# Key turns written in a row and read with a step by ScalarE, x of unit 1 copied by ScalarE, weight sums and one plain product moved, in a sparse attention and feed-forward kernel

## The chip, the cores and the metric

The kernel runs on one core of a Trainium2 chip. A core has five engines that run side by side: TensorE (PE in the profile; its weight loads are PEld) multiplies matrices into the accumulator memory PSUM, VectorE (DVE) and ScalarE (ACT) read PSUM and work element by element, GpSimd (POOL) works on the main on-chip memory, and SyncE (SP) issues transfers. Transfers (DMA) are issued from SyncE, ScalarE and GpSimd. The metric is the time of one execution on the device, in microseconds (us).

## What is computed

Attention over four batches of eight heads, 768 positions of 64 values. Each query sees the keys less than 16 positions away and, for each block of 32 positions, one summary key (the maximum over the block) that stands for 32. The result x feeds two layers with a sigmoid gate between them.

```python
k_sum = k.reshape(B, H, nb, block, D).max(axis=3)
v_sum = v.reshape(B, H, nb, block, D).mean(axis=3)
scores_l = scale * np.matmul(q, k.transpose(0, 1, 3, 2))
mask_l = np.abs(pos[:, None] - pos[None, :]) < window
scores_s = scale * np.einsum('bhsd,bhnd->bhsn', q, k_sum) + np.log(block)
...
x = attn_out.transpose(0, 2, 1, 3).reshape(B * S, H * D)      # 3072 x 512
h = x @ w_in                                                  # w_in 512 x 2048
out = (h * (1.0 / (1.0 + np.exp(-1.702 * h)))) @ w_out        # w_out 2048 x 512
```

## The kernel before

A **unit** is half a batch, 384 positions; there are eight, u = 0 to 7. The heads are taken as four **pairs** p, so that a pair fills 128 rows. Every engine keeps the order in which the program is written (the wrapper at line 28 sees to that, so nearly every row of the profile names line 28): what stands behind a waiting instruction on its engine waits too. The order is written out by hand.

**Start (lines 933 to 1028).** Twelve loads bring the keys of all four pairs (`kf`, half from SP and half from ACT) and the first half of their queries (`qf`). The build gives each load one of eight completion counters in turn, so the ninth and later loads are issued only when the load that last had their counter has landed. `exp_soon` makes ScalarE load its table for the exponential ahead of its first use. Then, for each pair, `cast_k` makes bf16 rows `kb`; `k_turn` transposes them with six matmuls of 128x128 against the identity `ident` into a bank pair `ps_k`; `k_own` copies that to the key array (`kx`), on ScalarE; `k_max` takes block maxima on VectorE. A load row holds three neighbouring positions (JH = 3), so the matmul of index r yields every third position, and `k_turn` writes its columns three words apart in PSUM, which puts positions in order. `q_turn` and `q_copy` do the same with queries (`ps_q`, `qT`): in the first half with the same stepped write, in the second half with a write in a row and a stepped write by VectorE's copy. `s_turn` makes scores in `ps_s`, `s_exp` their exponentials; `b_turn` and `b_exp` those of the block keys; `av_near`, `av_blocks` and `v_norm` the attention output, which `x_turn` transposes. `warmth` and `busy` are filler matmuls (`ps_w`). The fills of w_in, the second half of the queries and w_out are issued by GpSimd between its casts.

**A unit's feed-forward.** `ff_in` multiplies x transposed (`xT`, two halves of two pairs) with 16 column tiles of `w_in` (`ph`), and ScalarE puts the gate on each (`gT`). `ff_out` multiplies back with `w_out` (`po`): 12 calls of four matmuls, called slots 0 to 11. In unit 0 the slots run part by part of w_out (part 0 for three row tiles, then part 1, ...), so part 3 fills slots 9 to 11, and after each of these ScalarE copies the tile to `osb`. `beside(1, slot)` puts unit 1's attention between the slots, by the table `plan0`: q is a query turn, s scores of a pair, v the values of two pairs (with four norms on VectorE in all), x the transposes of two pairs by `tx` into `ps_x` with a copy to xT. `w_sums(c)` makes four sums of quarter-blocks of w_out on VectorE (`ta`, `tb`) for the fast matrix product (seven products instead of eight) used from unit 2 on. PSUM banks for `ph`, `po` and `ps_x` come from one ring of four (`mm`), so a new tile waits until the copy of the old one is done.

**The last units (`ff_in_pairs`, line 702).** Units 6 and 7 also do the first layer with seven products, M1 to M7, each two matmuls, for five pairs of column tiles, mixed with ten plain products of four matmuls into a bank L (`plain`). X, Y and V are banks; M5(i) adds to the bank X that VectorE reads for M6(i).

Of the kernel before, what the change touches and what calls it, by code (L numbers as in the profile page):

```python
# [35 lines left out]
def kernel(  # L36
# [16 lines left out]
    NP = H // 2  # L53
# [6 lines left out]
    HALF = S // 2  # L60
    TH = NQ // 2
    JH = NJ // 2

    pe = _Ordered(tc, nc.tensor)
    dve = _Ordered(tc, nc.vector)
    act = _Ordered(tc, nc.scalar)
# [207 lines left out]
    def copy(eng, out, in_):  # L274
        if eng is act:
            act.activation(out=out, in_=in_, func=ACT.Copy)
        elif eng == "dve_alone":

            dve.tensor_reduce(out=out, in_=in_.unsqueeze(len(in_.shape)), axis=AX.X, op=ALU.max)
        else:  # L280
            eng.tensor_copy(out=out, in_=in_)
# [94 lines left out]
    def at(ap, start, dims):  # L376
        a = ap[:, start:start + 1]
        return bass.AP(tensor=a.tensor, offset=a.offset, ap=[a.ap[0]] + dims)
# [24 lines left out]
    st = {}  # L403

    def k_turn(p):
        src = cast.pop(("k", p))
        big = st["K", p] = psb.tile([128, 1024], F32, name="ps_k", tag="big")
        for half in range(2):
            for r in range(JH):
                pe.matmul(out=at(big, half * 512 + r, [[JH, 128]]),  # L410
                          lhsT=src[:, half, r].rearrange("p h d -> p (h d)"),
                          rhs=ident, start=True, stop=True)

    def own_keys(p):
        return flat_kx(p, 1)[:, 0:S]

    def k_own(p, eng):

        copy(eng, own_keys(p).rearrange("p (e c) -> p e c", e=2),
             at(st["K", p], 0, [[512, 2], [1, HALF]]))  # L420

    def k_max(p):
        dve.tensor_reduce(out=ks0[p], in_=own_keys(p).rearrange("p (n c) -> p n c", c=block),
# [278 lines left out]
    def ff_in_pairs(u, early):  # L702

        (b11, b21), (b12, b22) = xTT
        xs = castp2.tile([128, 4, 2, HALF], F16, name="xsum", tag="kb")
        t = [xs[:, m] for m in range(4)]
        big = [psb.tile([128, 1024], F32, name="pw_in", tag="big") for _ in range(2)]
        mm = [pmm.tile([128, 512], F32, name="px_in", tag="mm") for _ in range(4)]
        X, V = ([m[:, 0:HALF] for m in mm[n:n + 2]] for n in (0, 2))
        Y = [big[0][:, n:n + HALF] for n in (0, 512)]  # L710
        L = big[1][:, 0:HALF]

        def gelu(w, f, src):
            act.activation(out=gT[w % 2][:, f, :], in_=src, func=ACT.Gelu_apprx_sigmoid)

        def one(w, f, ps):
            for ko in range(KO):
                pe.matmul(out=ps, lhsT=w_in_sb[:, ko, f * 128:(f + 1) * 128], rhs=xT[w % 2][ko],
                          start=(ko == 0), stop=(ko == KO - 1))
            gelu(w, f, ps)  # L720

        def prod(ps, a, b, i, first=False):
            for k in range(2):
                pe.matmul(out=ps, lhsT=a[:, k, i], rhs=b[:, k], start=(first and k == 0),
                          stop=(k == 1), skip_group_check=True)

        ws = [wt["s"][:, n] for n in range(4)]
        hold = {}

        def f0(i):  # L730
            return 2 * (NI - WI + i)

        def M1(i):
            x = X[i % 2]
            prod(x, wt[0, 0], b11, i, True)
            dve.tensor_copy(out=Y[i % 2], in_=x)

        def M7(i):
            v = V[i % 2]
            prod(v, ws[2], t[2], i, True)  # L740
            hold[i] = attp.tile([128, HALF], F32, name="m7", tag="x2")
            copy(act, hold[i], v)

        def M6(i):
            x = X[i % 2]
            prod(x, ws[1], t[1], i)
            dve.tensor_add(V[i % 2], x, hold[i])

        def M2(i):
            y = Y[i % 2]  # L750
            prod(y, wt[0, 1], b21, i)
            gelu(u, f0(i), y)

        def M5(i):
            x = X[i % 2]
            prod(x, ws[0], t[0], i)
            hold[i, 2] = attp.tile([128, HALF], F32, name="c22", tag="a_sb")
            dve.tensor_add(hold[i, 2], x, hold[i])

        def M4(i):  # L760
            v = V[i % 2]
            prod(v, wt[1, 1], t[3], i)
            gelu(u, f0(i) + 1, v)
            gelu(u + 1, f0(i) + 1, hold[i, 2])

        def M3(i):
            x = X[i % 2]
            prod(x, ws[3], b22, i)
            gelu(u + 1, f0(i), x)

        n, rest = 2 * (NI - WI), list(range(2 * (NI - WI)))

        def plain():
            one(u + 1, rest.pop(0), L)

        for f, ps in zip(range(n), (Y[0], X[1], V[1], L, Y[1], X[1])):
            if f == 2:
                M1(0)
            one(u, f, ps)
        dve.tensor_sub(t[2], b22, b12)  # L780
        dve.tensor_add(t[1], t[2], b11)
        dve.tensor_sub(t[0], b12, b11)
        dve.tensor_sub(t[3], b21, t[1])
        M2(0)
        M7(0)
        plain()
        M6(0)
        for i in range(1, WI):
            M1(i)
            for f in (M7, M5) if i == 1 else (M5, M7):  # L790
                f(i if f is M7 else i - 1)
            M4(i - 1)
            M6(i)
            M3(i - 1)
            M2(i)
            plain()
            if i == 2:
                early(0, NI - WI)
        i = WI - 1
        M5(i)  # L800
        M4(i)
        early(NI - WI, NI)
        plain()
        M3(i)
        assert not rest
# [123 lines left out]
    def exp_soon():  # L929
        act.activation(out=gate[:, 1:2], in_=gate[:, 0:1], func=ACT.Exp)  # L930


    dve.memset(gate, 0.0)
    for p in range(NP):
        load_k(p)
        load_q(p, 0)
    exp_soon()
    clear0(dve)
    dve.tensor_copy(out=identx, in_=ident)
    dve.memset(vs[:, :, D:VC], float(block))  # L940
# [102 lines left out]
    for p in range(NP):  # L1043
# [8 lines left out]
             6: ["v0", "s2", "s3"], 8: ["x0"], 9: ["v1", "S0", "S1"], 11: ["x1", "S2", "S3"]}  # L1052

    plan0 = {-1: ["q0", "q1"], 0: ["q2"], 1: ["q3"], 2: ["s0", "s1"], 4: ["s2", "s3"],
             7: ["v0", "v1"], 9: ["x0"], 11: ["x1"]}

    w51 = vw[1].rearrange("p (j e) h c -> p j e h c", e=2)

    def beside(u, slot):
        b, half = u // 2, u % 2  # L1060
        for what in (plan0 if u == 1 else plan1).get(slot, ()):
            i = int(what[1])
            if what[0] == "t":
                tq1(i, dve if i % 2 else act)
            elif what[0] == "q":
                q_turn(i, 1)
                q_copy(i, dve, 1)
            elif what[0] == "s":
                scores(b, half, i)
                if half and i == NP - 1:  # L1070
                    gelu_soon()
            elif what[0] == "S":
                scores(b, 1, i)
                if i == NP - 1:
                    gelu_soon()
            elif what[0] == "v":
                values(b, half, i, u == 1)
            else:
                tx(i, half)

    for u in range(2):
        todo = {}
        if u == 0:
            for p in range(NP):
                todo.setdefault(12 + p // 2, []).append(lambda p=p: cast_q(dve, p, 1))
        else:
            def value_rows():
                vsum(1, range(NJ))
                block_sums()
                halo_dmas(w51, 0)  # L1090
                sum_dmas(w51, 0)
                load_kc(2, range(6, H))
                load_vc(2)
                load_qc(2)

            todo = {0: [lambda: tk(0, 1)], 3: [lambda: tk(1, 1)], 5: [lambda: v_odd(1)],
                    9: [value_rows], 10: [lambda: tk(2, 1)], 13: [lambda: tk(3, 1)]}
            ff_in(u, range(3))
        for nt in range(0 if u else N0, NT):
            if u == 0 or nt > 2:  # L1100
                ff_in(u, (nt,))
            for f in todo.get(nt, ()):
                f()
        exp_soon()
        if u == 0:
            beside(1, -1)
            load_qc(1)
            load_kc(2, range(6))
        order = [(ms, part) for ms in range(JH) for part in range(4)]
        if u == 0:  # L1110

            order = [(ms, part) for part in range(4) for ms in range(JH)]
        for i, (ms, part) in enumerate(order):
            ff_out(u, ms, part)
            beside(u + 1, i)
            if u == 0 and i in (4, 7, 10):
                w_sums(i // 3 - 1)
            if u == 1 and i == 2:
                w_sums(3)
            if u == 1 and i == 3:  # L1120
                for g in range(2):
                    xk(g, 2)
# [22 lines left out]
    for b in range(1, B):  # L1145
# [3 lines left out]
        u = 2 * b  # L1149
# [95 lines left out]
```

The softmax here doesn't subtract the row's maximum and nothing guards it: scores larger than these inputs give would overflow.

## Time and profile before

| what | value |
|---|---|
| median of 6 runs | 208.75 us (208.21 to 209.3) |
| the profiled execution | 208.72 us |
| its span, first to last instruction | 207.0 us |
| TensorE matmuls | 199.8 us busy, 2212 |
| VectorE | 145.5 us busy |
| ScalarE | 123.7 us busy |
| GpSimd | 91.6 us busy |
| granted TensorE clock | 1.000 |
| HBM read, written | 27.26 MB, 6.29 MB |

The busy rows are times in which an engine has at least one instruction in work, as a share of the span. The difference of 1.7 us between the execution's time and the span lies around the span. In a row of the chain of waits stand the start, the length, the engine and the tile; the chain is followed back from the last instruction, at each step to what released it.

### The profile page before, as it was taken

How to read it: one execution, taken by the hardware profiler on the slowest of the kernel's cores; microseconds unless marked ns; L12 is line 12 of the kernel's file. 1: busy time of each engine (PE TensorE's matmuls, PEld its weight loads, DVE VectorE, ACT ScalarE, POOL GpSimd, SP SyncE). 2: the span in 40 equal slices, each digit the busy share in tenths (PEclk: the TensorE clock that was granted, in tenths of full speed). 3: DMA queues.
4: the chain of work that ended last, by engine and by line, in shares of the span. 5: the costliest groups of instructions: out<-in, count | busy, mean ns of one | idle time of the engine just before them, and what ended most of it. 6: DMA issues, size and time to landing. Idle time of an engine off the chain costs nothing.

```text
span 207.0 us, 5570 instructions
## 1 busy us (share of the span) xinstructions
PE 199.8 (97%) x2212; PEld 136.5 (66%) x2212; DVE 145.5 (70%) x421; ACT 123.7 (60%) x235; POOL 91.6 (44%) x162
## 2 busy tenths in 40 slices
PE   7899999998999999999999999999999999999992
PEld 3657555545665656566888865567887855668882
DVE  6687845696966679945757689579985956669431
ACT  0877676734685389677743657677626477881220
POOL 5995889399899943425999100402000000000000
PEclk9999999999999999999999999999999999999999
DMA  6999999999999999999999997993064260000323
GB/s 181 298 165 207 245 249 217 174 155 231 153 167 133 150 128 114 185 162 148 114 127 206 136 274 142 111 180 62 3 127 104 48 183 0 3 2 25 105 76 101
DMA packets 95009, 28.94 MB, mean 140 GB/s; under 512 B 82880, under 2 KB 92000, under 8 KB 94984
## 3 DMA queue, kind: packets, MB, share of 16 engines
q0 software_dynamic: 67920, 14.88, 81.7%
q1 hardware_dynamic: 25432, 12.53, 31.3%
q10 hardware_dynamic: 1632, 1.18, 1.9%
q8 instruction: 17, 0.28, 0.6%
q14 instruction: 8, 0.07, 0.1%
HBM read 27.26 MB, written 6.29 MB: 162 GB/s over the span
## 4 chain that ended last, share of the span: by engine, by line
PE 90%; DVE 6%; ACT 1%; issue 1%; DVEq 0%
PE ph L28 30%; PE px L28 15%; PE pw L28 8%; PE po L28 7%; PE px_in L28 6%; PE ps_av L28 4%; PE ps_s L28 4%; PE py L28 4%; PE pw_in L28 4%; PE ps_w L28 2%; PE ps_k L28 1%; PE ps_t L28 1%; DVE ta L28 1%; PE ps_x L28 1%; DVE x L28 1%; PE ps_q L28 1%
## 5 line engine op out<-in xcount | busy, mean ns | idle before, releaser
L28 PE MATMUL ph<-xT,w_in_sb 128*128 128x384 f16 x384 | 65.4, 326 | 1.2 <-DVE xT L28 1.2
L28 PEld LDWEIGHTS <-w_in_sb 128*128 128x128 f16 x462 | 44.3, 98 | 30.2 <-issue 1.5
L28 ACT ACTIVATE gT<-ph 128x384 f16<-128x384 f32 x96 | 45.7, 491 | 21.0 <-PE ph L28 20.8
L28 PEld LDWEIGHTS <-gT 128*128 128x128 f16 x384 | 36.1, 98 | 11.8
L28 ACT ACTIVATE a_sb<-ps_s 128x768 bf16<-128x768 f32 x28 | 21.1, 806 | 8.8 <-PE ps_s L28 8.7
L28 PE MATMUL po<-w_out_sb,gT 128*128 128x512 f16 x96 | 23.4, 380 | 0.0
L28 PEld LDWEIGHTS <-ss 128*128 128x128 f16 x216 | 20.7, 98 | 2.6
L28 ACT ACTIVATE t<-px 128x256 f32<-128x256 f32 x21 | 8.1, 384 | 21.9 <-PE px L28 21.9
L28 DVE TENSOR_TENSOR a_sb<-a_sb,mk 128x768 bf16<-128x768 bf16 x28 | 15.2, 555 | 7.5 <-ACT a_sb L28 6.4
L28 PE MATMUL pw<-tb,gT 128*128 128x256 f16 x144 | 18.7, 273 | 0.0
L28 PE MATMUL px<-ta,ss 128*128 128x256 f16 x144 | 18.7, 273 | 0.0
L28 ACT ACT_TABLE_LOAD x10 | 12.8, 1283 | 5.8 <-DMA kf<-in_k_dram 5.7
L28 DVE TENSOR_TENSOR x<-ps_av,rc 128x384 f16<-128x384 f32 x28 | 15.6, 557 | 1.0
L28 POOL DMA_DIRECT2D vw<-in_v_dram x18 | 15.9, 931 | 0.0
L28 POOL DMA_DIRECT2D vw<-vw x12 | 6.5, 563 | 20.5 <-DVE vw L28 18.1
L28 POOL DMA_DIRECT2D kb<-in_k_dram x16 | 13.2, 856 | 3.6 <-DMA w_out_sb<-in_moe_w_out_dram 3.2
L28 POOL DMA_DIRECT2D qb<-in_q_dram x16 | 13.3, 929 | 0.6 <-DMA vw<-in_v_dram 0.5
L28 DVE TENSOR_TENSOR osb<-pw,t 128x256 f32<-128x256 f32 x18 | 7.5, 421 | 8.6 <-PE pw L28 5.3
L28 DVE TENSOR_TENSOR ss<-gT 128x384 f16<-128x384 f16 (+4 forms) x18 | 7.5, 418 | 5.1 <-ACT gT L28 5.0
L28 PEld LDWEIGHTS <-kx 64*128 64x128 bf16 x400 | 7.2, 95 | 5.2 <-issue 4.0
L28 DVE TENSOR_REDUCE ks<-kx 128x24 bf16<-128x768 bf16 x8 | 7.6, 948 | 4.1 <-DMA kx<-kb 3.9
L28 PE MATMUL ps_s<-qT,kx 64*128 64x64 bf16 (+3 forms) x400 | 9.1, 190 | 0.3 <-DVE qT L28 0.2
(120 smaller groups left out, 312.7 us busy)
## 6 DMA issues: line engine op xcount, KB each, us to landing
out_dram<-osb SPq DMA_DIRECT2D x18, 256.0 KB, 4.3
vw<-in_v_dram POOLq DMA_DIRECT2D x18, 128.0 KB, 5.4
w_in_sb<-in_moe_w_in_dram POOLq DMA_DIRECT2D x4, 512.0 KB, 10.9
w_out_sb<-in_moe_w_out_dram POOLq DMA_DIRECT2D x4, 512.0 KB, 20.2
kb<-in_k_dram POOLq DMA_DIRECT2D x16, 96.0 KB, 5.1
qb<-in_q_dram POOLq DMA_DIRECT2D x16, 96.0 KB, 6.6
out_dram<-osb SPq DMA_DIRECT2D x12, 128.0 KB, 1.7
vw<-vs POOLq DMA_DIRECT2D x6, 148.5 KB, 3.9
```

Of the source, the lines that this page charges most:

```text
L28: r = f(*a, **kw)
```

## The change

Four edits. The key turns of the start write each matmul's 128 columns in a row, and ScalarE's copy reads them with a step of 128 words and puts positions in order. ScalarE's table load for the exponential is issued before its last two loads instead of after them. In unit 0's output layer, the copies of unit 1's x go to ScalarE, the second of them (x1) and the first weight sums move one slot forward. In the last units, one plain product moves from ahead of M6(0) to behind it.

```diff
     def k_turn(p):
...
-                pe.matmul(out=at(big, half * 512 + r, [[JH, 128]]),
+                pe.matmul(out=big[:, half * 512 + r * 128:half * 512 + (r + 1) * 128],
                           lhsT=src[:, half, r].rearrange("p h d -> p (h d)"),
                           rhs=ident, start=True, stop=True)
...
     def k_own(p, eng):
-        copy(eng, own_keys(p).rearrange("p (e c) -> p e c", e=2),
-             at(st["K", p], 0, [[512, 2], [1, HALF]]))
+        copy(eng, own_keys(p).rearrange("p (e c r) -> p e c r", e=2, r=JH),
+             at(st["K", p], 0, [[512, 2], [1, 128], [128, JH]]))
...
         M2(0)
         M7(0)
+        M6(0)
         plain()
-        M6(0)
...
-    for p in range(NP):
+    for p in range(NP - 1):
         load_k(p)
         load_q(p, 0)
     exp_soon()
+    load_k(NP - 1)
+    load_q(NP - 1, 0)
...
     plan0 = {-1: ["q0", "q1"], 0: ["q2"], 1: ["q3"], 2: ["s0", "s1"], 4: ["s2", "s3"],
-             7: ["v0", "v1"], 9: ["x0"], 11: ["x1"]}
+             7: ["v0", "v1"], 9: ["x0"], 10: ["x1"]}
...
-                tx(i, half)
+                tx(i, half, act if u == 1 else dve)
...
-            if u == 0 and i in (4, 7, 10):
+            if u == 0 and i in (3, 7, 10):
                 w_sums(i // 3 - 1)
```

## The prediction

> **What bounds the kernel now.** I read the page's busy shares first, then who TensorE waited for, then the chain of waits through each place that came up, then tiles and transfers at those places.
>
> ```profile
> PE 199.8 (97%) x2212; PEld 136.5 (66%) x2212; DVE 145.5 (70%) x421; ACT 123.7 (60%) x235; POOL 91.6 (44%) x162
> ```
>
> ```profile
> PE ph L28 <- DVE xT L28: 1.2, 2, 0.8
> PE ps_k L28 <- DVE kb L28: 0.4, 1, 0.4
> PE ps_s L28 <- DVE qT L28: 0.2, 1, 0.2
> ```
>
> A TensorE at 97% says little (matmuls overlap and their ends are modelled). The waits say more: in 207 us TensorE waits for another engine four times after its first instruction (behind the arrow: sum, count, longest), and the largest sum is for xT on VectorE. So most of the kernel is TensorE's own stream, and time is to be had only where that stream is stretched. The chain shows three such places.
>
> ```profile
> 4.86 1.28 PE ps_k L28 x6
> 6.14 0.32 PE ps_w L28 x3
> ...
> 12.59 0.66 PE ps_k L28 x6
> ...
> 32.01 0.34 PE ps_q L28 x6
> ...
> 45.71 0.47 DVE xT L28
> ...
> 47.64 0.48 DVE xT L28
> ...
> 48.16 1.14 PE ph L28 x6
> ```
>
> First place, the start: six key turns take 1.28 us (213 ns each), while three filler matmuls of the same 128x128 shape right behind take 0.32 (107). Later, when TensorE runs at about twice the pace (the granted clock shows 1.0 throughout), six key turns take 0.66 (110) and six query turns of the second half 0.34 (57). What sets the two apart is the write: the slow ones write every third PSUM word, the fast ones a row. The half-0 query turns also write every third word (0.65 for three at 6.46) and stay so. Second place: from 37.9 to 48.2 us the chain leaves TensorE and runs on VectorE: masks, three weight sums of 1.5 us each, four norms, two copies of x. Third place:
>
> ```profile
> 170.61 0.34 PE px_in L28 x2
> ...
> 171.04 0.58 DVE px_in L28
> 171.66 1.62 PE px_in L28 x8
> ```
>
> Here a product of the last unit waits until VectorE has read the bank that it adds to.
>
> **The change, part by part.**
>
> *The plain product behind M6(0).* Matmuls follow each other every 0.163 us here. Before, starts are 171.09, 171.26, then 171.66 instead of 171.42: M5(0) adds to the bank that VectorE reads for M6(0) until 171.61. With the plain product's four matmuls (0.65) between them, M6(0) starts 0.65 earlier, VectorE's addition waits for ScalarE's m (170.06 + 0.48) and ends near 171.1, before 171.42. M6(0)'s input sum is ready at 169.24, before its new start at 169.79. The plain product is covered by nothing and costs nothing: the same four matmuls stand elsewhere. Gain **0.24**; what is late next is M3(0) (0.16, there already).
>
> *x copies to ScalarE, x1 and the first weight sums a slot earlier.* TensorE ends its transposes at 45.67 (45.34 plus six of 0.055) and could go on; it starts the input products at 46.23, and their second half at 48.16, not 47.21. Lost: 0.55 + 0.95 = **1.50**. In the changed order ScalarE runs, from 43.48: osb 0.60, x0 0.805, osb 0.60, x1 0.805, osb 0.60, so x0 is there at 44.89 and x1 at 46.29 at the latest. TensorE now does the x1 transposes before the last four output matmuls and starts the input products at the same 45.67; it needs x0 at once, and x1 and its bank for the third tile at 45.67 + 4 x 0.163 = 46.33. Both fit, x1 by 0.04. In the built order the bank of the third output tile, which is copied last, is not waited for until the fourth tile. VectorE must have the last norm done before x1's transposes at 44.5: norms start when the values are there (41.1) and take 4 x 0.69, so 43.8. The first weight sums (1.56) now stand before the masks of s2 and s3: these end near 40.4 rather than 40.0; the values that need them start at 41.1. The chunks of w_out that the sums wait for are there. Gain 1.45 to 1.50; **1.49** taken. If ScalarE were 0.3 slower, 0.26 of it is lost.
>
> Here a rule stands against the change. The Trainium skill, "ScalarE: Activation LUTs", section Rules for kernel authors, gives plain arithmetic to VectorE, "not ScalarE". The rows agree on the price:
>
> ```profile
> L28 ACT ACTIVATE xT<-ps_x x5: 472/492/805, 20.2 to 82.2; 128x384 f16<-128x384 f16 x3, 128x768 f16<-128x768 f16 x2
> L28 DVE COPY xT<-ps_x x5: 357/552/558, 22.0 to 74.7; 128x768 f16<-128x768 f16 x4, 128x384 f16<-128x384 f16 x1
> ```
>
> By the rule alone the two copies lose 2 x 0.25 = 0.5 us. But ScalarE is idle 2.55 before its first osb and 2.5 after the last, and VectorE is the chain, so I go by the chain: +1.49, not -0.5.
>
> *Key turns in a row.* TensorE saves 6 x 0.106 = 0.64 on the first pair and 6 x 0.053 = 0.32 on each of three others. Not all of it lies on the path, as VectorE is busy without a break from 7.1 to 14.0. The first query copy on VectorE moves from 7.14 to 6.50; but the next cast needs a load issued at 1.84 that takes 5.3, so at 7.14, where it started at 7.61. The cast after it took 1.32 instead of 0.35, and ended at 9.20 just after GpSimd's issue of the v loads (to 9.01). If it is held to 9.2 again, VectorE gains nothing there, and what remains is TensorE's own: three turns of pair 2 (0.16), six of pair 3 (0.32), less small waits: 0.37 by 15.5 us. If it slips through, the stage is up to 1.4 shorter. Either way a ceiling waits:
>
> ```profile
> w_out_sb<-in_moe_w_out_dram POOLq DMA_DIRECT2D x1, 512.0 KB, 17.0
> ```
>
> Issued at 14.73, it lands at 31.73; the first output product starts at 32.18. That leaves 0.45. I take **0.40** for the start.
>
> *The strided read on ScalarE.* No row shows ScalarE reading PSUM with a step. Contiguous it takes 811 ns for 768. Bounds: no change (a gain has no reason), or twice, 1.6 us. The second is the rule of "PSUM — Partial Sum Buffer", Specifications, that lines have 8 bytes and broken patterns slow matmuls much, carried over to a reader; the trace shows it for TensorE's writes (107 to 213). But TensorE's strided writes reach a word per 0.86 ns (110 for 128), and ScalarE reads no faster when contiguous: its rows of 1024 and 768 elements, 1024 and 806 ns, differ by 0.85 ns an element. So I take no change. At 1.6, ScalarE's row of four copies and three exponentials becomes the path: the first stage then ends 0.2 later than before instead of 0.4 earlier.
>
> *The table load before the last two loads.* ScalarE's first key copy can start near 6.05 (its last issue) instead of 7.08; the scores behind it wait for the query copy too, so I count nothing. The price is order: the build lets a ninth load wait for an earlier one's landing, and which one changes. k of pair 3 now waits until 5.23 (was issued at 4.08), q of pair 3 until about 5.65 (5.27). Landing 5.7 and 5.9 later: 11.0 and 11.55. VectorE casts that k at 12.02: 1 us of cover. GpSimd casts that q at 11.20: 0.35 late, and its w_in, q and w_out issues after it. They then lie 10 to 21 us in a full queue, so I cost this at 0; without that cover the 0.45 above shrinks to 0.1.
>
> **Sum.** 0.40 + 1.49 + 0.24 = 2.13. The profiled execution took 208.72 (span 207.0 and 1.7 around it); the median of the runs is 208.75, so no correction: **206.6**. Later transfers allow it: the last v rows for the block sums land near 52.4 (needed 54.4 - 1.9), the sum rows at 65.0 (67.5 - 1.9), the transposed queries at 96.7 (100.0 - 1.9).
>
> **The rivals.** *Loads are the floor.* The page shows the DMA at 9 in nearly all slices to 135 us, and margins of 0.1 to 0.6 above are thin; against it, TensorE waits for no load now. The start's 0.4 is lost and 0.2 at 52: 207.2. *ScalarE at twice the price*: 1.73 - 0.2, so 207.2. *Slower*: ScalarE's strided read costs far more than twice. Its fourth key copy ends at about 8.1 + 4c for a cost c (6.05, a cast, two exponentials, four copies); the block scores of pairs 2 and 3 at 17.9 need it 0.94 earlier. The loss passes the 1.73 gained elsewhere from c = 2.65, over three times the row; at four times (3.2) it is 4.1 lost, 211.1. Nothing in the trace speaks for that much. *It doesn't do what it says*: the gap at 46 to 48 stays, because x1 on ScalarE comes behind the osb copies; then 208.1.
>
> **How the numbers follow.** Forecast 0.66 (206.2 to 207.0); loads 0.10; twice 0.10; gap stays 0.06; slower 0.05; and 0.03 for a tie between. A measurement of this kernel tells 0.2% (0.4 us) from no change. All but the last two cases are faster, 0.92; I move 0.02 of it to slower for what I don't see: faster 0.90, within 0.03, slower 0.07. Range 205.9 to 207.5: below, the start comes through whole if w_out lands earlier; above, both middle rivals.
>
> **What would show it.** Six key turns at 0.34 when fast; key copies on ScalarE at 0.81; no wait of ph for xT; starts 0.163 apart at M5(0); first po 0.4 earlier, and if it waits for w_out, the ceiling. Wrong if key copies exceed 1.6 us, or TensorE waits for loads between 50 and 100 us.

## The result, and the profile after

| | before | after |
|---|---|---|
| median of all runs | 208.7 us (208.13 to 209.51, 38 runs) | 207.41 us (206.39 to 210.38, 17 runs) |
| the profiled execution | 208.72 us | 207.41 us |
| its span | 207.0 us | 205.7 us |

The ratio is 0.9934, with a 95% interval of 0.9919 to 0.9948: 1.4 us gained (1.1 to 1.7), where the forecast said 2.1. The median, 207.41, lies inside the range of 205.9 to 207.5, but only 0.1 under its upper end. The ratios here and below leave out a few longer runs with a lower granted clock (0.984 to 0.992), and are not exactly those of the medians. The busy line of the changed kernel, and four lines of its list of what TensorE waited for:

```profile
PE 197.2 (96%) x2212; PEld 134.4 (65%) x2212; DVE 143.3 (70%) x419; ACT 124.9 (61%) x237; POOL 91.4 (44%) x162
```

```profile
PE ps_k L28 <- DVE kb L28: 1.0, 3, 0.4
PE ps_av L28 <- issue: 0.6, 1, 0.6
PE ps_q L28 <- POOL qb L28: 0.5, 1, 0.5
PE ps_av L28 <- DMA vw<-vs: 0.5, 2, 0.3
```

The wait of `ph` for `xT` (1.2 before) is gone. The waits of the key turns for `kb` grew from 0.4 to 1.0. Four entries are new. Two are at the start: for queries that GpSimd casts (`qb`), and for keys that ScalarE copies (`kx`, 0.4, not shown). `issue` is a stall that no other engine ends. The last is a wait of TensorE for a transfer, which the profile before does not have: the values of unit 1 (`ps_av`) wait for the rows of v's block sums (`vw<-vs`, called the sum rows from here on).

The places in order of time. First the start: the six key turns of pair 0 and of pair 3, from the timeline of TensorE of the changed kernel (start, length, operation).

```profile
4.40 0.63 PE L28 MATMUL ps_k<-ident,kb 128*128 128x128 bf16 x6
4.87 0.33 PE L28 MATMUL ps_w<-warm 128*128 128x128 bf16 x3
...
11.52 0.60 PE L28 MATMUL ps_k<-ident,kb 128*128 128x128 bf16 x6
```

Six turns now take 0.47 us from their first start to the next instruction's. Before it was 1.19 (4.66 to 5.85):

```profile
4.66 1.49 PE L28 MATMUL ps_k<-ident,kb 128*128 128x128 bf16 x6
5.85 0.61 PE L28 MATMUL ps_w<-warm 128*128 128x128 bf16 x3
```

Not all of this is the edit. In this execution TensorE's pace had already doubled: the three fillers behind the key turns last 0.33, before 0.61. In e1, the same kernel in another execution, the fillers still start 0.107 apart, and the six turns take 0.64 (4.66 to 5.30). At the same pace the write in a row thus saves 0.55. The last pair begins 0.86 earlier than before (11.52 and 12.38), and the last scores of the start (`s_turn(3)`) 1.03 earlier (14.49 and 15.52). Little of this arrives:

```profile
18.34 0.54 PE L28 MATMUL ps_av<-vb,a 128*128 128x65 bf16 x13 [0.62 <-issue]
...
31.35 0.50 PE L28 MATMUL ps_q<-ident,qb 128*128 128x128 bf16 x6
31.96 1.04 PE L28 MATMUL po<-w_out_sb,gT 128*128 128x512 f16 x4
```

After the stall (in brackets) the lead is 0.49: the query turns start at 31.35, before at 31.84. The first output product starts at 31.96 instead of 32.18, so 0.22 is left. It follows the query turns by 0.61 where it followed by 0.34 before: w_out's first quarter, issued at 14.53, landed 17.4 later, at 31.93.

At the gap everything came as forecast. The timeline of TensorE of the changed kernel:

```profile
44.25 0.50 PE L28 MATMUL ps_x<-identx,x 128*128 128x128 f16 x6
44.58 1.03 PE L28 MATMUL po<-w_out_sb,gT 128*128 128x512 f16 x4
45.44 2.11 PE L28 MATMUL ph<-xT,w_in_sb 128*128 128x384 f16 x12
47.39 0.50 PE L28 MATMUL ps_t<-ident,kb 128*128 128x128 bf16 x6
```

The transposes of x1 stand before the last output product, and twelve input products run in a row, with no bracket. The key transposes behind them start at 47.39; before, at 49.13:

```profile
49.13 0.50 PE L28 MATMUL ps_t<-ident,kb 128*128 128x128 bf16 x6
```

The lead grows from 0.22 to 1.74.

Then part of it is lost. The chain of waits of the changed kernel in the stretch from 54 to 68 us:

```profile
55.93 6.29 DMA kq<-in_k_dram
...
62.85 3.53 DMA vw<-vs
66.38 0.14 issue
66.52 0.54 PE ps_av L28 x22
67.06 0.46 PE ps_s L28 x24
```

Here the chain no longer runs on TensorE. GpSimd issues the second half of the sum rows at 62.85, after a wait of 1.65 for a key load of batch 2 that it issued at 55.93; before, it issued them at 61.64. They land at 66.38 (before 65.04), and the values need them 1.7 earlier than before. That wait is not the whole cause: the first half, issued at 60.53 as before (60.54), took 5.5 to land instead of 4.3, so at 66.0 it is late too. TensorE loses 0.71 here.

Last, the plain product behind M6(0), on TensorE:

```profile
168.44 0.81 PE L28 MATMUL px_in<-xsum,wsum 128*128 128x384 f16 x4
169.09 0.81 PE L28 MATMUL pw_in<-xT,w_in_sb 128*128 128x384 f16 x4
169.74 0.49 PE L28 MATMUL px_in<-xT,w_in_sb 128*128 128x384 f16 x2
170.06 0.81 PE L28 MATMUL px_in<-xsum,wsum 128*128 128x384 f16 x4
```

All starts are 0.16 apart per matmul; the gap at M5(0) is gone, and the lead grows by 0.30. The sum over the places is 0.22 + 1.52 + 0.30 - 0.71 = 1.33, which is the difference of the spans (207.0 - 205.7 = 1.3).

### The profile page after: what moved, and what is told of

The parts are those of the page before. It is cut to its first block, busy times and chain, and to the rows that moved or that the text cites. A ratio compares the mean times of both kernels' runs of the same rounds, so it can differ in the third digit from the quotient of the medians.

```text
span 205.7 us, 5570 instructions
## 1 busy us (share of the span) xinstructions
PE 197.2 (96%) x2212; PEld 134.4 (65%) x2212; DVE 143.3 (70%) x419; ACT 124.9 (61%) x237; POOL 91.4 (44%) x162
## 3 DMA queue, kind: packets, MB, share of 16 engines
HBM read 27.26 MB, written 6.29 MB: 163 GB/s over the span
## 4 chain that ended last, share of the span: by engine, by line
PE 66%; DMA 21%; POOL 9%; issue 1%; SPq 0%; DVE 0%; POOLq 0%
PE ph L28 20%; PE px L28 16%; DMA w_out_sb<-in_moe_w_out_dram 10%; PE pw L28 8%; PE px_in L28 6%; DMA w_in_sb<-in_moe_w_in_dram 4%; PE py L28 4%; PE pw_in L28 4%; POOL qb L28 3%; DMA kq<-in_k_dram 3%; PE ps_av L28 3%; POOL vw L28 3%; PE ps_s L28 2%; PE po L28 2%; DMA qf<-in_q_dram 2%; POOL vb L28 2%
## 5 line engine op out<-in xcount | busy, mean ns | idle before, releaser
L28 PE MATMUL pw<-tb,gT 128*128 128x256 f16 x144 | 18.7, 273 | 0.0
L28 PE MATMUL px<-ta,ss 128*128 128x256 f16 x144 | 18.7, 273 | 0.0
L28 POOL DMA_DIRECT2D vw<-vw x12 | 6.5, 561 | 19.0 <-DVE vw L28 15.2
L28 DVE RECIPROCAL rc<-ps_av 128x6 f32<-128x6 f32 x32 | 6.0, 188 | 5.7 <-PE ps_av L28 5.4
## 6 DMA issues: line engine op xcount, KB each, us to landing
vw<-vs POOLq DMA_DIRECT2D x6, 148.5 KB, 4.5
```

Of the source, the lines that this page charges most:

```text
L28: r = f(*a, **kw)
```

## The experiments

Theory from this reading: the three edits do on TensorE what was forecast, but **transfers** take back about 0.7 to 0.9 us, at w_out's first quarter (32 us) and at the sum rows (66 us). Rivals: the start's gain is lost to TensorE's own stall at 18.3 us; or the forecast gains were not there at all, and only one of the edits works. In the tables the ratio is to the runs of the kernel before on the same chip (medians 208.98 beside e1 to e4, 208.79 beside e5 to e8, 208.77 beside e9 to e12).

### The sum rows on another queue: e1 to e4

e1 is the changed kernel again; e2 and e3 issue the sum rows and their neighbours from SP, in the changed kernel and in the one before:

```diff
-                halo_dmas(w51, 0)
-                sum_dmas(w51, 0)
+                halo_odd(w51, 0, sp)
+                halo_even(w51, 0, sp)
+                sum_dmas(w51, 0, sp)
                 load_kc(2, range(6, H))
```

e4 is e2 with the load of the second half of the queries cut in two, w_out's first quarter issued between the halves, and the casts of pairs 2 and 3 moved behind the query copies:

```diff
-    for p in range(NP):
-        load_q(p, 1)
-    for c in range(4):
+    load_q(0, 1)
+    load_q(1, 1)
+    load_w_out(0)
+    load_q(2, 1)
+    load_q(3, 1)
+    for c in range(1, 4):
         load_w_out(c)
```

> The changed kernel unaltered, as the measure for the three kernels beside it. Theory (late rows): near 207.4, and its times scatter by 1 us and more, since TensorE waits near 66 us for rows of v that pass through a full transfer queue. Rival (plain noise): the same 207.4, but the scatter has no wait in the profile that goes with it.

> The changed kernel with the six transfers of the halo and sum rows of unit 2's v issued by SP instead of GpSimd, where they stood behind six key loads and waited for one of them to land. Late rows: the wait of 0.7 us at slot 6 of unit 1 goes, the time falls to about 206.7, and the scatter shrinks to that of the kernel before (about 1 us over all runs instead of 2). Rival (all transfers share the same engines and are the floor): the rows land as late as before or the key loads behind them do, and the time stays within 0.2 of the changed kernel.

> The kernel before with the same six transfers on SP. Late rows: TensorE did not wait there before (rows at 65.0, needed at 67.5), so nothing is gained: 208.7, within 0.2. Rival (SP is just the better queue for these rows, or GpSimd's queue relieved of them speeds the loads behind): 208.2 or less.

> As the one with rows on SP, and the load of the second half of the queries split in two, with the first quarter of w_out between the halves, and the casts of pairs 2 and 3 behind the first two query copies. Theory (w_out's first quarter is the ceiling of the start): it lands about 2 us before it is needed, the first output product starts at 31.7 instead of 31.96, and the time is 0.25 lower than with rows on SP alone. Rival (the start's gain is lost before, near 18 us, where TensorE stood 0.6 us for nothing that shows): no change, within 0.1. It is slower by up to 0.5 if the later casts of the queries hold up the third query turn.

| | median us (runs) | ratio, interval | TensorE's waits for transfers in the profile |
|---|---|---|---|
| e1 | 207.88 (10) | 0.9933, 0.9907 to 0.9959 | w_out 1.1 |
| e2 | 208.52 (22) | 0.9969, 0.9950 to 0.9988 | w_out 1.5 |
| e3 | 209.34 (14) | 1.0010, 0.9988 to 1.0032 | w_out 0.4, sum rows 0.2 |
| e4 | 208.22 (22) | 0.9965, 0.9945 to 0.9985 | sum rows 0.9 |

The repeat has the same ratio, but not the same profile: this execution did not wait for the sum rows, it waited at w_out.

The remedy missed its expectation: in e2 the wait for the sum rows is gone, and the time is not better than e1's, by its median worse. The wait at w_out in e2 lies over 20 us ahead of the moved rows, so the edit did not put it there; and with TensorE late by it (values at 67.12), this profile does not test whether the rows come earlier. e4 does. There the wait for w_out is gone and the first output product starts at 31.7, as expected, but the wait for the sum rows is back at 0.9, though they are issued from SP. From the chain of e4:

```profile
58.63 8.75 DMA vw<-vs
```

SP issued the second half 4 us earlier than GpSimd did in the changed kernel (62.85), and it landed 1.0 later, at 67.38: it was under way for 8.75 us instead of 3.53. In e3 it was 9.07. Why rows from SP take longer was not tried. A limit that all transfers share would fit, and is not shown by this.

Two more things follow. One profile is one sample: where loads land differs between executions of the same program. And e3 shows no gain from the rows on SP where TensorE is not ahead.

### One edit at a time: e5 to e9

e5 has the edits of the start alone, e6 those of x and the weight sums alone, e7 the plain product alone; e9 is e6 and e7 together. e8 is the changed kernel with the copies of unit 1's x back on VectorE:

```diff
-                tx(i, half, act if u == 1 else dve)
+                tx(i, half)
```

> The kernel before with the key turns in a row, the stepped read on ScalarE and the earlier table load, and nothing else. Ceiling theory: TensorE is about 1.0 us ahead at 14.5 us, but the first output product waits for w_out's first quarter, so 0.2 to 0.3 is left at 32 us and at the end: 208.45. Rival (the start comes through): 207.7.

> The kernel before with unit 1's x copied by ScalarE, x1 and the first weight sums a slot forward, and nothing else. Theory: the gap of 1.5 us at 46 to 48 closes, ScalarE's copies show 0.80, and since TensorE is 1.5 and not 1.74 ahead at slot 6 of unit 1, it waits there 0.3 to 0.5 for the sum rows: 207.4 to 207.6. Rival (the rows land on time when the start is not moved): 207.2.

> The kernel before with the one plain product moved behind M6(0). Theory: M5(0) no longer waits, 0.25 to 0.3 less, nothing behind it can eat it: 208.45. Rival (a wait takes its place at M3(0) or at the bank L): 208.7.

> The changed kernel with the two copies of x back on VectorE, x1 and the weight sums still a slot forward. If ScalarE's copies carry the gain: the gap comes back whole, 208.7 or so. If the order carries it: VectorE ends the norms at 43.8 and the second weight sums at 45.3, then copies x0 by 45.9 and x1 by 46.4, so TensorE waits 0.45 for x0 and not for x1: up to 0.45 over the changed kernel, less if the wait for the sum rows behind it takes part of it up (it would then be within 0.2).

> The kernel before with the edits of x, the weight sums and the plain product; the start (key turns, table load) is that of before. If the start brings nothing because loads and a stall take it up: 207.4, as the changed kernel, ratio to before 0.992 to 0.995. If the start brings the 0.40 that was forecast: 207.8, ratio 0.9955. Expected 207.45.

| | edits | median us (runs) | ratio, interval |
|---|---|---|---|
| e5 | start | 208.87 (14) | 0.9995, 0.9973 to 1.0017 |
| e6 | x and weight sums | 207.76 (22) | 0.9951, 0.9931 to 0.9971 |
| e7 | plain product | 208.62 (14) | 0.9995, 0.9975 to 1.0014 |
| e8 | all, x copied by VectorE | 207.50 (15) | 0.9935, 0.9915 to 0.9954 |
| e9 | all but the start | 207.58 (22) | 0.9941, 0.9921 to 0.9961 |

The start alone brings nothing that can be measured; nor does its absence cost anything that can: e9 is at 0.9941 where the whole change is at 0.9934. The intervals, about half a microsecond either way, do not exclude the 0.40 that was forecast. The edit of x carries the gain, 1.0 us of the 1.4. The plain product alone (0.1 us by its ratio) is below what its interval can tell.

e8 says which half of that edit it is. With the copies on VectorE and only the order changed, two lines of its list of waits are

```profile
PE ps_av L28 <- DMA vw<-vs: 0.3, 1, 0.3
PE ph L28 <- DVE xT L28: 0.3, 1, 0.3
```

Of the 1.2 for `xT`, 0.3 is left. The time is the changed kernel's. So the **order** (x1 ahead of the last output product, the weight sums ahead of the masks) makes the gain; its two moves were not tried apart. The move to ScalarE is worth at most the remaining 0.3 on TensorE, and nothing of it shows in the times.

The start, seen over all these profiles. w_out's first quarter is issued at the same place in the program in all of them (in e4 it is not, and it is left out); issue and landing are from the list of that tile's instructions. The first three columns of times follow TensorE: the last scores of the start, the matmul at which it goes on after the stall near 18 us, and the query turns ahead of the first output product.

| start of | profile | last scores | goes on | query turns | w_out issued | lands | first output product |
|---|---|---|---|---|---|---|---|
| before | before | 15.52 | 18.83 | 31.84 | 14.7 | 31.7 | 32.18 |
| | e6 | 15.23 | 18.59 | 31.61 | 14.7 | 31.5 | 31.94 |
| | e3 | 15.05 | 18.61 | 31.62 | 15.3 | 32.4 | 32.50, waited 0.4 |
| | e7 | 15.25 | 18.59 | 31.61 | 15.5 | 32.8 | 32.81, waited 0.7 |
| | e9 | 15.18 | 18.32 | 31.42 | 15.5 | 32.9 | 32.90, waited 1.0 |
| after | after | 14.49 | 18.34 | 31.35 | 14.5 | 31.9 | 31.96 |
| | e5 | 14.90 | 18.32 | 31.33 | 14.9 | 31.3 | 31.67 |
| | e8 | 14.45 | 18.34 | 31.35 | 15.2 | 31.6 | 31.69 |
| | e1 | 14.30 | 18.09 | 31.10 | 15.0 | 32.6 | 32.69, waited 1.1 |
| | e2 | 14.57 | 18.34 | 31.34 | 15.4 | 33.2 | 33.30, waited 1.5 |

By the medians of the five profiles each, the new start leads by 0.74 at the last scores (14.49 and 15.23), by 0.25 behind the stall (18.34 and 18.59), and by 0.27 at the query turns (31.34 and 31.61). So most of its gain is lost at the stall, before any wait for a transfer. What is left meets a landing that goes from 31.3 to 33.2, whichever start the kernel has, and cannot be seen through that.

The stall is at the same matmul in all 14 profiles, those of before and of e10 to e12 included: behind the third of a block of values, where starts otherwise lie 0.03 apart, 0.10 to 0.85 us pass. In each of them a 16 KB packet of the kind `instruction` (the first on queue q8) has landed 1.2 to 1.5 us before TensorE goes on. It landed between 16.7 and 18.7, and TensorE went on between 18.1 and 20.1, later where the packet was later. In five profiles with the new start (after, e2, e4, e5, e8) it went on at 18.32 to 18.34, whether it had started the third matmul at 17.49 or at 17.94: coming earlier gained nothing. A wait for instructions to be loaded would fit. The profile does not say whose instructions the packet holds, and no run moved it, so the cause is not shown.

### Fewer bytes, and another order of loads: e10 to e12

If transfers take the gain back, it must come out where there are fewer of them. e10 and e11 leave out one load, 768 KB, ahead of w_out in the queue, in the kernel before and in the changed one:

```diff
-            if half:
-                pool.dma_start(out=early[1].rearrange("p i h r d -> p (i h) (r d)"),
-                               in_=q[0, :, HALF:S].rearrange("h (p r) d -> p h (r d)", r=JH))
...
-             raw["q", p, half])
+             raw["q", p, 0])
```

e12 computes everything, and moves the first six key loads of batch 2 behind the sum rows:

```diff
             load_qc(1)
-            load_kc(2, range(6))
...
                 sum_dmas(w51, 0)
-                load_kc(2, range(6, H))
+                load_kc(2)
```

> The kernel before without the load of the second half of batch 0's queries (768 KB); the casts for that half read the first half's queries, so that half of the output is another. At the mean 195 GB/s these bytes take 4 us, so what is queued behind them (w_out, the rows of unit 1) should land some 4 us earlier until the queue has caught up. In the profile of before TensorE waits for no load, so both theories expect no change here: 208.7, at most 0.4 less.

> The changed kernel with the same load left out. Theory that loads are the floor: TensorE no longer waits for the sum rows at 66 (0.7) nor stands near w_out at 32 (0.2 and more), and the whole forecast appears: 206.5, 2.1 under e10. Rival, that the start's gain is lost to TensorE's own stall at 18.3 and the rest is not due to loads: 207.2 to 207.5, 1.3 under e10.

> The changed kernel with six heads' key loads of batch 2 (384 KB as bf16, 768 KB read) issued behind the sum rows of unit 1 and no longer ahead of them. Theory that the sum rows waited for these loads: GpSimd issues the rows at about 61.2 without a wait, they land near 65, the wait at 66 (0.7) is gone and w_out's landing at 32 is not touched, since these loads are issued behind it: 206.8, ratio 0.990. Rival, that the wait only moves, to the key or query rows of batch 2 at 80 to 100 us: 207.4 as the changed kernel.

| | median us (runs) | ratio, interval |
|---|---|---|
| e10 | 208.72 (14) | 1.0000, 0.9975 to 1.0026 |
| e11 | 206.74 (6) | 0.9899, 0.9870 to 0.9928 |
| e12 | 206.97 (7) | 0.9921, 0.9889 to 0.9953 |

The kernel before doesn't notice the missing load, within half a microsecond. The changed one gains by it: e11 is 1.98 us under e10, close to the 2.13 of the forecast's sum. (The one profile of e10 is its slowest execution, 210.15 us; no time is read from it but those of the stall.) The list of waits of e11:

```profile
PE ps_k L28 <- DVE kb L28: 0.8, 2, 0.6
PE ps_av L28 <- issue: 0.5, 1, 0.5
PE ps_q L28 <- POOL qb L28: 0.5, 1, 0.5
PE ps_s L28 <- DVE qT L28: 0.4, 1, 0.4
PE ps_s L28 <- ACT kx L28: 0.4, 1, 0.4
```

No transfer stands in it, and the stall at 18 us does, at 0.51. The timeline of TensorE in e11 at the three places:

```profile
31.43 1.03 PE L28 MATMUL po<-w_out_sb,gT 128*128 128x512 f16 x4
...
43.73 0.50 PE L28 MATMUL ps_x<-identx,x 128*128 128x128 f16 x6
...
65.26 0.57 PE L28 MATMUL ps_av<-vw,a_sb 128*64 128x65 bf16 x24
```

The first output product starts 0.75 ahead of before (32.18), with w_out landed by 29.5 (13.5 + 16.0). At the values the lead is 2.26 (67.52 before), where the changed kernel has 1.0. So a lead does arrive at 32 us once w_out does not hold it. How much of the 0.75 is the start's is open: the query turns of before (31.84) are the latest of the five profiles with the old start, those of e11 (31.09) are 0.3 to 0.5 ahead of the other four, and the load left out also spares GpSimd an issue ahead of w_out's. The intervals of e11 and of the changed kernel (0.9919 to 0.9948) still overlap by a little; the step from the one to the other rests on the traces as much as on the times.

In e12 the sum rows are issued earlier than I expected, at 56.52 and 57.33: six issues fewer stand before them on GpSimd, 4.95 us in the changed kernel (six loads of 96 KB each, more bytes than the expectation says). The timeline of GpSimd in e12, and then of TensorE:

```profile
56.52 0.65 POOL L28 DMA_DIRECT2D vw<-vs  x1
57.33 0.62 POOL L28 DMA_DIRECT2D vw<-vs  x1 [0.16 <-issue]
57.97 0.86 POOL L28 DMA_DIRECT2D kq<-in_k_dram  x1
...
66.03 0.57 PE L28 MATMUL ps_av<-vw,a_sb 128*64 128x65 bf16 x24
```

The values start at 66.03 with no wait, and the moved key loads bring no new wait in that profile. Its query turns start at 31.87, no earlier than before, so its 1.7 us (span 205.3) come from the other two places alone. By its median e12 is the fastest kernel of the study that computes the whole, 206.97, as forecast for it (206.8). Its interval includes the changed kernel's ratio, so that it beats the changed kernel is likely but not shown.

## Why the prediction was right, and where it was too large

**The range held by a small margin.** The forecast's own value, 206.6, was 0.8 too low. What carried the range up to 207.5 were two rivals, both at 207.2. *Loads are the floor* had the right mechanism. *ScalarE at twice the price* did not: its number is near the measured one by luck.

**Right in direction and in its largest term.** The gap at 46 to 48 us was put at 1.49 and measured 1.52 in the trace. Its steps held: x0 and x1 copied in 0.80 and 0.81 us, the weight sums ahead of the masks, the norms done at 43.9, no wait of `ph` for `xT`. Putting the chain above the rule that plain arithmetic belongs on VectorE did no harm, and e8 shows that it decided little: most of the gain came from the order, which either engine can serve.

**The plain product** was put at 0.24 and measured 0.30 in the trace, too small for a run of its own.

**The stepped read** was right at "no change": four copies of 768 values took 802 to 812 ns, before 792 to 811. The rival of twice the price is out, and the slower one with it. The line width that the Trainium skill, "PSUM — Partial Sum Buffer", Specifications, gives for broken patterns bears on TensorE's writes here (107 against 213 ns) and not on this reader.

**The key turns** of the last pair take 0.60 us from the first start to the end of the last, before 0.86 (the lengths in the timelines at 11.52 and 12.38): 0.26 saved of the 0.32 put down for them. On the first pair 0.55 was saved at the same pace (e1), where 0.64 stood; the 0.72 of the profile has TensorE's early change of pace in it, which is luck.

**The table load** moved the first key copy on ScalarE from 7.08 to 6.41, and ended in no measurable gain with the rest of the start.

**What failed** is the sentence that closes the sum: "Later transfers allow it: ... the sum rows at 65.0 (67.5 - 1.9)". I took landing times out of one profile as fixed, and compared them to needs that move. The margin was 0.6, and the sum rows landed 1.2 to 1.3 later than in that profile: the second half because GpSimd's issue waited 1.65 for an earlier load, the first because it was longer under way. Cost: 0.71 in the profiled execution. It is also what the prediction named as a sign of being wrong, a wait for loads between 50 and 100 us. The rival "loads are the floor" placed the loss at 32 and 52 us and got a chance of 0.10, with the reason that TensorE waits for no load now. That reason was one profile too: e3, e7 and e9, with the old start, waited 0.4 to 1.0 at w_out. A landing that goes over 1.9 us from profile to profile deserved more.

The second mis-sized term is the start, 0.40. Its ceiling was named (w_out at 31.73), and the profile gives 0.22; but over the profiles the ceiling itself moves between 31.3 and 33.2, and e5 and e9 find nothing. The stall at 18 us is a second ceiling, which the prediction did not have: it leaves about 0.3 of a lead of 0.7. The old start has this stall too, shorter (0.28 in the profile before, start to start, where the changed kernel has 0.81).

Left open: what the stall is; no run took it away. Whether the wait at w_out comes from the queue's length or from the time at which the loads ahead of it are issued was not tried either.

## What to carry to other kernels

When the memory queues are full, a landing time in one profile is a sample: before a gain is counted, compare the margin at every transfer behind the edit with the spread of its landing, and with the time at which its issuing engine can get to it. An edit that lets TensorE run ahead should come with a look at what stands in front of the next needed rows in the issue order; moving loads that are needed late behind rows that are needed soon took the wait away here (its gain in time is likely, not shown), and another queue did not. And when an engine is idle next to a wait, try the order before the engine: x1 and the weight sums one slot earlier brought nearly everything, the change of engine little.

## What the runs showed of the hardware

- A step of 128 words in ScalarE's read of PSUM costs nothing (802 to 812 ns for 768 values, in a row 792 to 811), while a step of three words in TensorE's write doubles a matmul of 128 columns (57 to 110 ns, or 107 to 213). Transposing in a row and putting the order right in the reader is therefore free for the reader.
- The same program landed the same load at different times: w_out's first quarter took 17.4 us in one profile of the changed kernel and 17.6 in the other, from issues 0.5 us apart; over the ten profiles of the table 16.4 to 17.8.
- In all 14 profiles TensorE stands 0.10 to 0.85 us at the same matmul, put down to no engine and no transfer, and goes on 1.2 to 1.5 us after the first 16 KB packet of the kind `instruction` on queue q8 has landed. Its cause was not shown.
- Sum rows of 148.5 KB issued by SP were under way for 8.75 and 9.07 us (e4, e3); issued by GpSimd, for 3.4 to 5.5 (before, after, e1, e8, e11, e12).
- Leaving 768 KB of 27.26 MB out changed the kernel before by nothing that the interval shows, and the changed kernel by 0.7 us (the intervals overlap by a little): the same bytes are free or not, by how far TensorE runs ahead.
